# Decode attention over a 64K-key cache: earlier statistics for the second half of a pair, its accumulator in another bank, and one V load in halves

## The chip, the cores and the metric

The kernel runs on one core of a Trainium2 chip. The metric is device time in microseconds (us) from the first to the last instruction of an execution, as measured on the device; lower is better. One execution in each run is also recorded by the hardware profiler. Its span (660.0 us for the kernel before) is about 1.3 us shorter than that execution's time.

Engine names: PE is the matmul engine, DVE the vector engine, ACT the scalar engine, POOL the general engine, SP the engine that issues the DMAs here. PE's clock is throttled in some stages: 0.5 in the profile means half speed.

## The reference

One new token attends to a cache of 65,536 keys with 32 query heads that share 8 key/value heads; beside it runs a small dense layer, and both are added to the input.

```python
def _A_ref(x, k_cache, v_cache, wq, wo):        # x: (1, 1, 512); caches: (1, 8, 65536, 128) bf16
    q = (x @ wq) ...                            # 32 heads of 128
    k = jnp.repeat(k_cache, 4, axis=1); v = jnp.repeat(v_cache, 4, axis=1)
    scores = jnp.einsum("bhqd,bhkd->bhqk", q, k) * (128 ** -0.5)
    p = softmax(scores, axis=-1)
    o = jnp.einsum("bhqk,bhkd->bhqd", p, v)
    return o.transpose(...).reshape(...) @ wo
# out = x + _A_ref(layernorm(x), ...) + dense_gelu(layernorm(x), ...)
```

The caches are 268 MB, and each byte is used once for four query heads. All inputs together are 280.5 MB.

## The kernel before

The keys of one kv head are cut into four units of 16,384. Two units make a pair; there are 16 pairs, run as a rolled loop. One K chunk and one V chunk per pair, 8.4 MB each, come by DMA. K has two buffers. V has only one, of two halves ("Va" and "Vb"), so the V chunk of the next pair can be issued only when this pair's PV matmuls have read the old one.

```python
    for i in range(NU // 2):
        chunks += [("Ka", i), ("Kb", i)] if i in (0, LASTP - 1, LASTP) else [("K", i)]
        chunks += [("Va", i), ("Vb", i)] if i == LASTP else [("V", i)]
    chunks += [("W", 0)]                        # wo, the output projection
    ...
    def issue_chunks():                         # strictly in the order of the list
        while next_chunk[0] < len(chunks):
            ...
            if not need <= free:                # a buffer that it needs is still in use:
                return                          # nothing behind it is issued either
            ...                                 # one DMA; a POOL memset per half marks its landing ("flag")
```

One pair: 32 groups of 8 K tiles are transposed on PE, copied from PSUM to SBUF by DVE or ACT, and multiplied with q. Then come the row maxima over all keys ("statistics": two tiny matmuls with small DVE steps between), four exponentials on ACT with their sums, and the PV matmuls of both units.

```python
        for f in range(2 * FPU - LAG, 2 * FPU):
            scores(f)
        pv(2 * i, 0, 40)                # first unit's PV, tiles 0 to 39 of 128
        stats_1()                       # second unit's statistics, first matmul
        pv(2 * i, 40, 92)
        stats_2(2 * i + 1)              # second matmul, gives the negated maximum
        for j in range(HPG):
            weights(2 * i + 1, j)       # four exponentials on ACT, with sums
        keep_max(i)
        ...                             # (last pair only)
        pv(2 * i, 92, TPD)
        keep_sums(i)                    # DVE: the sums into one table
        total()                         # matmul with ones over all 128 columns of it
        ...                             # (last pair only)
        pv(2 * i + 1, 0, TPD)           # second unit's PV; then V's buffer is free
```

Both PVs accumulate in columns of one PSUM bank, `pO`. Because `keep_sums` waits for the four exponentials and `total` for `keep_sums`, PE stands still between the two PVs.

## Time and profile before

| | kernel before |
|---|---|
| median of 3 runs | 662.28 us (661.1 to 662.54) |
| profiled span | 660.0 us |
| load queue, share of 16 DMA engines' span | 98.8% |
| PE busy | 81% |
| usual time between two chunk landings | 19.36 us per 8.4 MB |

First, lines of the profile's page: the span; the engines' busy times; GB/s in 40 equal slices; and two DMA queues with their packets, MB and share of the 16 engines' span. q1 is the load queue, q8 brings instructions.

```profile
span 660.0 us, 29018 instructions
...
PE 535.0 (81%) x12682; PEld 509.0 (77%) x12682; DVE 280.4 (42%) x574; ACT 250.0 (38%) x454; POOL 5.6 (1%) x75
...
GB/s 388 439 463 415 369 445 409 417 445 445 445 441 385 445 445 445 445 417 409 445 445 437 441 409 429 445 433 433 409 441 421 433 437 425 421 445 413 425 441 271
...
q1 hardware_dynamic: 6600, 280.50, 98.8%
q8 instruction: 8, 0.13, 0.1%
...
```

The load queue is busy nearly all the time. The GB/s row tells more than the average: the fifth slice, 66 to 82 us, has 369, most others 409 to 445.

Next, POOL's timeline (start, duration, engine, line, operation, what ended the idle time before it). Each line marks the landing of a chunk.

```profile
...
80.49 0.12 POOL L454 MEMSET flag<- 1x1 bf16 x2 [19.22 <-DMA kv<-in_A_k_cache_dram]
101.61 0.12 POOL L454 MEMSET flag<- 1x1 bf16 x2 [20.99 <-DMA kv<-in_A_v_cache_dram]
...
509.30 0.12 POOL L454 MEMSET flag<- 1x1 bf16 x2 [19.23 <-DMA kv<-in_A_k_cache_dram]
529.83 0.12 POOL L454 MEMSET flag<- 1x1 bf16 x2 [20.41 <-DMA kv<-in_A_v_cache_dram]
549.20 0.12 POOL L454 MEMSET flag<- 1x1 bf16 x2 [19.24 <-DMA kv<-in_A_k_cache_dram]
...
```

V of pair 1 (the second line) came 21.1 us after K of pair 1, and V of pair 12 (at 529.83) came 20.5 us after the K chunk before it; the K chunk after it (549.20) came in the usual 19.37.

Then two V issues from SP's timeline, and one 5 us window (columns: length, busy time and instruction count of PE, PE weight load, DVE, ACT and POOL; PE clock; DMA share; GB/s).

```profile
...
79.84 0.33 SPq L449 DMA_DIRECT2D kv<-in_A_v_cache_dram  x1
...
505.69 0.33 SPq L449 DMA_DIRECT2D kv<-in_A_v_cache_dram  x1
...
```

```profile
...
75.00:80.00 5.00, 3.61 (x129) 3.47 (x127) 0.05 (x1) 0.00 (x0) 0.00 (x0) 0.50 0.61 257
...
```

V of pair 1 is issued at 79.84 us, when K of pair 1 is all but landed (80.49). Nothing else is queued, and the DMA share falls to 0.61. At 505.69 us the V issue is 3.6 us ahead of the K landing at 509.30.

PE's own waits (what waited, for what: us in total, times, longest), and the PV stage of pair 14 in PE's timeline:

```profile
...
PE pst L597 <- POOL flag L454: 65.9, 14, 6.8
PE pA L735 <- DVE sums_all L708: 19.3, 16, 1.2
...
```

```profile
...
608.68 0.35 PE L645 MATMUL pss<-q_cur,kt_ring 128*128 128x4 bf16 x8 [0.54 <-ACT kt_ring L636]
608.89 1.15 PE L718 MATMUL pO<-P_bf,kv 128*128 128x4 bf16 x40
609.98 0.59 PE L672 MATMUL pA<-ident_f,pmax 128*4 128x128 f32 x2
610.49 1.54 PE L718 MATMUL pO<-P_bf,kv 128*128 128x4 bf16 x52
611.97 0.59 PE L683 MATMUL pA<-diag,ones_f 4*128 4x4 f32 x2
612.49 1.12 PE L718 MATMUL pO<-P_bf,kv 128*128 128x4 bf16 x36
614.81 0.79 PE L735 MATMUL pA<-sums_all,ones_f 128*128 128x128 f32 x2 [1.20 <-DVE sums_all L708]
615.39 3.60 PE L718 MATMUL pO<-P_bf,kv 128*128 128x4 bf16 x128
...
```

PE waits 65.9 us for chunks, mostly for K, so the loads are the bound. Within a pair it waits 0.5 us for the last score tile's copy (line 608.68) and 1.2 us for the sums (line 614.81). The whole PV stage, from 608.89 to the end of the last matmul at 619.0, takes 10.1 us.

### The profile page before, as it was taken

What the parts mean: (1) busy time and instruction counts of PE and PEld (TensorE: products, weight loads), DVE (VectorE), ACT (ScalarE), POOL (GpSimd) and SP (SyncE); (2) the same over time, 40 slices, a digit from 0 to 9 for tenths busy, and PEclk for the clock granted to TensorE, in tenths of its full rate; (3) what the DMA queues carried; (4) which work ended last, traced back from release to release, by engine and by line L of the source; (5) the groups of instructions that cost most, each with busy time, mean ns of one, the idle gap of its engine ahead of it and who ended that gap; (6) DMA issues with size and microseconds to landing.
All of it is one profiled execution on the core that took longest, in us unless ns stands there. A gap on an engine that the chain in (4) does not pass through costs nothing. (4 is left out here: it accounts for less than half of the span.)

```text
span 660.0 us, 29018 instructions
## 1 busy us (share of the span) xinstructions
PE 535.0 (81%) x12682; PEld 509.0 (77%) x12682; DVE 280.4 (42%) x574; ACT 250.0 (38%) x454; POOL 5.6 (1%) x75
## 2 busy tenths in 40 slices
PE   2488498696969879697987959888696986999997
PEld 0277497696959879697987959788696986999997
DVE  3245063352615436162543616345261633536363
ACT  0144053352614425152442515345161543535261
POOL 0000000000000000000000000000000000000000
PEclk9689597795968769596886959679595976969695
DMA  9999899999998999999999999999999999999996
GB/s 388 439 463 415 369 445 409 417 445 445 445 441 385 445 445 445 445 417 409 445 445 437 441 409 429 445 433 433 409 441 421 433 437 425 421 445 413 425 441 271
DMA packets 6759, 280.66 MB, mean 425 GB/s; under 512 B 858, under 2 KB 1372, under 8 KB 1500
## 3 DMA queue, kind: packets, MB, share of 16 engines
q1 hardware_dynamic: 6600, 280.50, 98.8%
q8 instruction: 8, 0.13, 0.1%
q10 hardware_dynamic: 148, 0.01, 0.0%
q14 instruction: 3, 0.02, 0.0%
HBM read 280.50 MB, written 0.00 MB: 425 GB/s over the span
## 5 line engine op out<-in xcount | busy, mean ns | idle before, releaser
L597 PE MATMUL pst<-ident_bf,kv 128*128 128x128 bf16 x4096 | 336.6, 233 | 69.3 <-POOL flag L454 65.9
L597 PEld LDWEIGHTS pst<-ident_bf,kv 128*128 x4096 | 262.8, 105 | 71.4 <-issue 71.2
L636 ACT ACTIVATE kt_ring<-pst 128x1024 bf16<-128x1024 bf16 x192 | 196.7, 1025 | 310.9 <-PE pst L597 294.7
L634 DVE COPY kt_ring<-pst 128x1024 bf16<-128x1024 bf16 x320 | 216.8, 691 | 200.3 <-PE pst L597 200.2
L645 PE MATMUL pss<-q_cur,kt_ring 128*128 128x4 bf16 x4096 | 173.1, 165 | 10.9 <-ACT kt_ring L636 8.6
L645 PEld LDWEIGHTS pss<-q_cur,kt_ring 128*128 128x128 bf16 x4096 | 154.0, 97 | 16.2 <-ACT kt_ring L636 10.0
L718 PEld LDWEIGHTS pO<-P_bf,kv 128*128 128x128 bf16 x4096 | 115.5, 102 | 12.6 <-issue 11.3
L718 PE MATMUL pO<-P_bf,kv 128*128 128x4 bf16 x4096 | 118.4, 166 | 6.2 <-issue 6.2
L696 ACT ACTIVATE P_bf<-pss,negm 128x128 bf16<-128x128 f32 x128 | 57.2, 544 | 69.5 <-DVE negm L686 69.5
L728 DVE COPY o_all<-pO 128x4 f32 (+1 forms) x32 | 5.2, 162 | 77.8 <-PE pO L718 77.0
L696 ACT ACTIVATION_READ_ACCUMULATOR P_bf<-pss,negm 128x1 f32 x128 | 35.0, 273 | 0.0
L653 DVE TENSOR_REDUCE pmax<-pss 128x4 f32<-128x512 f32 x32 | 21.9, 686 | 25.2 <-PE pss L645 25.2
L735 PE MATMUL pA<-sums_all,ones_f 128*128 128x128 f32 x32 | 12.7, 501 | 19.3 <-DVE sums_all L708 19.3
L735 PEld LDWEIGHTS pA<-sums_all,ones_f 128*128 128x128 f32 x32 | 8.0, 311 | 20.6 <-DVE sums_all L708 20.6
L686 DVE TENSOR_SCALAR negm<-pA 128x4 f32<-128x4 f32 x32 | 5.0, 157 | 26.8 <-PE pA L683 26.8
L672 PE MATMUL pA<-ident_f,pmax 128*4 128x128 f32 x64 | 13.6, 299 | 1.3
L683 PE MATMUL pA<-diag,ones_f 4*128 4x4 f32 x64 | 14.3, 291 | 0.0
L674 DVE TENSOR_REDUCE gmax<-pA 4x1 f32<-4x128 f32 x32 | 8.8, 274 | 11.6 <-PE pA L672 11.6
L683 PEld LDWEIGHTS pA<-diag,ones_f 4*128 4x128 f32 x64 | 11.5, 223 | 1.9
L526 PE MATMUL pA<-ones_bf,xn_row 1*128 1x1 bf16 x4 | 0.3, 174 | 12.4 <-DVE xn_row L522 12.4
L526 PEld LDWEIGHTS pA<-ones_bf,xn_row 1*128 1x128 bf16 x4 | 0.2, 116 | 12.4 <-DVE xn_row L522 12.4
L454 POOL MEMSET flag<- 1x1 bf16 x64 | 4.2, 91 | 641.0 <-DMA kv<-in_A_k_cache_dram 327.7
(78 smaller groups left out, 60.2 us busy)
## 6 DMA issues: line engine op xcount, KB each, us to landing
kv<-in_A_k_cache_dram SPq DMA_DIRECT2D x6, 4096.0 KB, 36.6
kv<-in_A_v_cache_dram SPq DMA_DIRECT2D x2, 4096.0 KB, 26.3
kv<-in_A_wq_dram SPq DMA_DIRECT2D x1, 4096.0 KB, 12.5
kv<-in_B_w_dram SPq DMA_DIRECT2D x2, 1792.0 KB, 17.9
kv<-in_A_wo_dram SPq DMA_DIRECT2D x1, 2048.0 KB, 33.0
kv<-in_A_wo_dram SPq DMA_DIRECT2D x1, 1024.0 KB, 35.1
kv<-in_A_wo_dram SPq DMA_DIRECT2D x1, 512.0 KB, 35.8
kv<-in_A_wo_dram SPq DMA_DIRECT2D x1, 384.0 KB, 36.3
```

Source lines behind the costliest of these rows:

```text
L597: ins = pe.transpose(pst[tb][:, at * 128:(at + 1) * 128], kslot[0][:, t, :], ident_bf[:, :]).ins
L634: e, fn = DVE, lambda tb=tb, dst=dst: dve.tensor_copy(out=dst, in_=pst[tb][:, :])
L636: e, fn = ACT, lambda tb=tb, dst=dst: act.activation(out=dst, in_=pst[tb][:, :], func=ACTF.Copy)
L645: lambda k=k, kb=kb, at=at, t=t: pe.matmul(pss[k][:, at:at + HPG], lhsT=kt_ring[:, kb * FCOL + t * 128:kb * FCOL + (t + 1) * 128], rhs=q_c ...
L653: lambda k=k: dve.tensor_reduce(out=pmax[:, :], in_=pss[k][:, 0:CW].rearrange("p (t j) -> p j t", j=HPG), axis=AX.X, op=ALU.max),
L672: sch.op(PE, lambda: pe.matmul(pA[0:HPG, PA_ST:PA_ST + 128], lhsT=pmax[:, 0:HPG], rhs=ident_f[:, :], start=True, stop=True), reads=["pmax" ...
L674: sch.op(DVE, lambda: dve.tensor_reduce(out=gmax4[:, :], in_=pA[0:HPG, PA_ST:PA_ST + 128], axis=AX.X, op=ALU.max), reads=["pA"], writes=[" ...
L683: sch.op(PE, lambda: pe.matmul(pA[:, PA_SB:PA_SB + HPG], lhsT=ones_f[0:HPG, 0:128], rhs=diag4[0:HPG, 0:HPG], start=True, stop=True), reads ...
L696: lambda: act.activation(out=P_v[k][:, :, j], in_=src[:, :, j], func=ACTF.Exp, bias=negm[:, at:at + 1], scale=1.0, accum_out=sums[:, at:at ...
L718: lambda k=k, t=t: pe.matmul(pO[:, os], lhsT=vslot[:, k * TPD + t, :], rhs=P_v[k][:, t, :], start=t == 0, stop=t == TPD - 1),
L728: sch.op(DVE, lambda: dve.tensor_copy(out=o_all[:, at_pair(i, PW, k * HPG, HPG)], in_=pO[:, os]), reads=[f"pO{k}"], writes=[f"o{k}"])
L735: sch.op(PE, lambda: pe.matmul(pA[:, PA_SUM:PA_SUM + NC], lhsT=ones_f[:, :], rhs=sums_all[:, :], start=True, stop=True), reads=["ones_f", ...
```

## The change

The intent is to end a pair sooner on PE, so that V's buffer is free sooner, and to close the gap at the second V chunk:

- The second unit's statistics run at tiles 24 and 48 of the first PV instead of 40 and 92, so the exponentials are done when the first PV ends.
- The second PV accumulates in another bank (`pA`) and starts at once. The sums are totalled per pair by a matmul of 8 columns instead of 128, placed behind 32 tiles of the second PV.
- V of pair 1 comes in halves, so that its first half can be issued after the first PV of pair 0.
- The copy of the last score tile goes to DVE instead of ACT.

```diff
-        chunks += [("Va", i), ("Vb", i)] if i == LASTP else [("V", i)]
+        chunks += [("Va", i), ("Vb", i)] if i in (1, LASTP) else [("V", i)]
 ...
-        if f % 8 in (0, 2, 3, 5, 6):
+        if f % 8 in (0, 2, 3, 5, 7):            # these copies on DVE, the others on ACT
 ...
     def pv(u, t0, t1):
+        acc, res = ((pO, "pO0"), (pA, "pA"))[k]
 ...
-                    pO[:, os], lhsT=vslot[:, k * TPD + t, :], rhs=P_v[k][:, t, :],
+                    acc[:, 0:HPG], lhsT=vslot[:, k * TPD + t, :], rhs=P_v[k][:, t, :],
 ...
-    def total():
-        sch.op(PE, lambda: pe.matmul(pA[:, PA_SUM:PA_SUM + NC], lhsT=ones_f[:, :], rhs=sums_all[:, :], ...
+    def total(i):
+        sch.op(PE, lambda: pe.matmul(pO[:, PO_SUM:PO_SUM + PW], lhsT=ones_f[:, :], rhs=sums[:, :], ...
+        keep_o(i, 0)                            # DVE: first unit's result out of pO
+        sch.op(DVE, lambda: dve.tensor_copy(out=tot_all[:, ...], in_=pO[:, PO_SUM:PO_SUM + PW]), ...
 ...
-        pv(2 * i, 0, 40)
+        pv(2 * i, 0, 24)
         stats_1()
-        pv(2 * i, 40, 92)
+        pv(2 * i, 24, 48)
         stats_2(2 * i + 1)
 ...
-        pv(2 * i, 92, TPD)
-        keep_sums(i)
-        total()
+        pv(2 * i, 48, TPD)
+        pv(2 * i + 1, 0, 32)
+        total(i)
 ...
-        pv(2 * i + 1, 0, TPD)
+        pv(2 * i + 1, 32, TPD)
```

The rest of the diff (cut) passes exact semaphore growth per turn to the code that rolls the loop, and renames the table of sums.

More of the change, by code (lines that the diff above doesn't have):

```diff
@@ L152, in dma, with _fold @@
         return ev
-def _fold(bodies):
+def _fold(bodies, each):
     n = len(bodies)
@@ L164, in _fold @@
                 seen.setdefault((k, s), {})[i] = v
-    growth = {}
+    growth = dict(each)
     for (_, s), at in seen.items():
         if n - 1 in at and n - 2 in at:
-            growth.setdefault(s, at[n - 1] - at[n - 2])
+            assert growth.setdefault(s, at[n - 1] - at[n - 2]) == at[n - 1] - at[n - 2]
     out = []
@@ L193, in _emit, with _emit_rolled @@
             ins.then_inc(pub[0], pub[1])
-def _emit_rolled(eng_obj, ops, marks, holder=None, step=None):
-    folded, growth = _fold([ops[a:b] for a, b in zip(marks, marks[1:])])
+def _emit_rolled(eng_obj, ops, marks, each, holder=None, step=None):
+    folded, growth = _fold([ops[a:b] for a, b in zip(marks, marks[1:])], each)
     _emit(eng_obj, ops[:marks[0]])
@@ L369, in bass_parallel_sum__gqa_block_cached__dense_activation_gelu__decode_kernel @@
     negm_all = sb("negm_all", [128, NC], F32)
-    sums_all = sb("sums_all", [128, NC], F32)
+    tot_all = sb("tot_all", [128, NC], F32)
     o_all = sb("o_all", [128, NC], F32)
@@ L394, in bass_parallel_sum__gqa_block_cached__dense_activation_gelu__decode_kernel @@
     PA_ST = 128
-    PA_SUM = 384
+    PO_SUM = HPG
     csem = [sch.dsem(f"csem{i}") for i in range(6)]
@@ L404, in bass_parallel_sum__gqa_block_cached__dense_activation_gelu__decode_kernel @@
     sem_out = sch.dsem("dout")
-    sch.op(POOL, lambda: pool.memset(sums_all[:, :], 1.0), writes=["sums_all"])
     for t, res in ((ident_bf, "ident_bf"), (ident_f, "ident_f")):
@@ L705, in keep_max @@
                reads=["negm0", "negm1"], writes=["negm_all"])
-    def keep_sums(i):
-        sch.op(DVE, lambda: dve.tensor_copy(out=sums_all[:, at_pair(i, PW, 0, PW)], in_=sums[:, :]),
-               reads=[f"sums{at}" for at in range(PW)], writes=["sums_all"])
     def pv(u, t0, t1):
@@ L713, in pv @@
         x = "ab"[k]
-        os = slice(k * HPG, (k + 1) * HPG)
+        acc, res = ((pO, "pO0"), (pA, "pA"))[k]
         for t in range(t0, t1):
@@ L718, in pv @@
                 lambda k=k, t=t: pe.matmul(
-                    pO[:, os], lhsT=vslot[:, k * TPD + t, :], rhs=P_v[k][:, t, :],
+                    acc[:, 0:HPG], lhsT=vslot[:, k * TPD + t, :], rhs=P_v[k][:, t, :],
                     start=t == 0, stop=t == TPD - 1),
-                reads=[f"V{i}{x}"] + [f"P{k}_{j}" for j in range(HPG)], writes=[f"pO{k}"],
+                reads=[f"V{i}{x}"] + [f"P{k}_{j}" for j in range(HPG)], writes=[res],
                 publish=t == TPD - 1,
@@ L727, in pv, with keep_o @@
         done_chunk(f"V{x}")
-        sch.op(DVE, lambda: dve.tensor_copy(out=o_all[:, at_pair(i, PW, k * HPG, HPG)], in_=pO[:, os]),
-               reads=[f"pO{k}"], writes=[f"o{k}"])
+        if k:
+            keep_o(i, k)
+    def keep_o(i, k):
+        acc, res = ((pO, "pO0"), (pA, "pA"))[k]
+        sch.op(DVE, lambda: dve.tensor_copy(out=o_all[:, at_pair(i, PW, k * HPG, HPG)], in_=acc[:, 0:HPG]),
+               reads=[res], writes=[f"o{k}"])
     def by_head(t, a, b):
         return t[:, a * GW:b * GW].rearrange("p (g c j) -> p g j c", c=CPG, j=HPG)
-    def total():
-        sch.op(PE, lambda: pe.matmul(pA[:, PA_SUM:PA_SUM + NC], lhsT=ones_f[:, :], rhs=sums_all[:, :],
-                                     start=True, stop=True), reads=["ones_f", "sums_all"], writes=["pA_sum"])
+    def total(i):
+        sch.op(PE, lambda: pe.matmul(pO[:, PO_SUM:PO_SUM + PW], lhsT=ones_f[:, :], rhs=sums[:, :],
+                                     start=True, stop=True),
+               reads=["ones_f"] + [f"sums{at}" for at in range(PW)], writes=["pO0"])
+        keep_o(i, 0)
+        sch.op(DVE, lambda: dve.tensor_copy(out=tot_all[:, at_pair(i, PW, 0, PW)], in_=pO[:, PO_SUM:PO_SUM + PW]),
+               reads=["pO0"], writes=["tot_all"])
     def heads(t, a, b):
@@ L750, in weigh_2 @@
     def weigh_2():
-        sch.op(DVX, lambda: dve.tensor_tensor(out=wtot[:, :], in0=coef[:, :], in1=pA[:, PA_SUM:PA_SUM + NC],
-                                              op=ALU.mult), reads=["coef", "pA_sum"], writes=["wtot"])
+        sch.op(DVX, lambda: dve.tensor_tensor(out=wtot[:, :], in0=coef[:, :], in1=tot_all[:, :],
+                                              op=ALU.mult), reads=["coef", "tot_all"], writes=["wtot"])
         sch.op(DVX, lambda: dve.tensor_reduce(out=heads(rden, 0, G), in_=by_head(wtot, 0, G), axis=AX.X,
@@ L822, in bass_parallel_sum__gqa_block_cached__dense_activation_gelu__decode_kernel @@
         sch.reads.setdefault(res, []).extend(sch.reads["va"])
-    for res in ("K1a", "K1b", "Va", "Vb", "pO0", "pO1"):
+    for res in ("K1a", "K1b", "Va", "Vb", "pO0"):
         sch.reads.setdefault(res, []).append(made)
@@ L837, in bass_parallel_sum__gqa_block_cached__dense_activation_gelu__decode_kernel @@
         assert not (DVE.pending or ACT.pending)
+        was = {e.sem: e.count for e in (PE, DVE, ACT)}
         body(i)
+        each = {e.sem: e.count - was[e.sem] for e in (PE, DVE, ACT)}
     marks.append(len(PE.ops))
@@ L902, in _ @@
         def _(e):
-            _emit_rolled(e, ACT.ops, [m[1] for m in marks2])
+            _emit_rolled(e, ACT.ops, [m[1] for m in marks2], each)
         @block.vector
         def _(e):
-            _emit_rolled(e, DVE.ops[:rest[DVE]], [m[0] for m in marks2], pair)
+            _emit_rolled(e, DVE.ops[:rest[DVE]], [m[0] for m in marks2], each, pair)
         @block.tensor
@@ L911, in _ @@
             k_setup()
-            _emit_rolled(e, PE.ops[:rest[PE]], marks, step=k_step)
+            _emit_rolled(e, PE.ops[:rest[PE]], marks, each, step=k_step)
     for e, obj in ((PE, pe), (DVE, dve), (SP, sp)):
```

## The prediction

> **What bounds it now.** The DMA stream. The queue table puts the load queue at 98.8% of 16 engines' span, 280.5 MB. The K/V flags (timeline of the flag memsets, set when each 8.4 MB chunk lands) mostly come every 19.36 us, 433 GB/s. The Trainium skill, "DMA: Bandwidth & Descriptors", Specifications, gives a 435 GB/s fabric ceiling; the trace agrees. So the bytes alone cost about 647 us (estimate). PE is 81% busy but waits for a flag in 14 of 16 pairs (waits view: 65.9 us), so its time matters only where it delays a DMA issue, and in the last three pairs, which it runs almost without a break.
>
> **Where the stream loses time.**
> 1. Once it runs dry. V of pair 1 is issued at 79.84 us, when pair 0's PV has ended (SP timeline); K1 lands at 80.44; in 75 to 80 us the DMA share is 0.61 (windows view). V1's flag comes at 101.61, 1.6 us late for the last DMA engine, up to 3.6 us for others. Pair 0's PV is slow because PE stands still 5.0 us at 66 us and 1.2 us at 77 us ("issue"). My reading is instruction fetch in the loop's first turn (the skill, "Runtime: NRT & Kernel Launch", Instruction fetch mechanics, describes fetches by DMA and stalls on them; the trace shows the stall, not its cause).
> 2. Four later V chunks take 19.8 to 20.6 us (flags at 334, 374, 530, 609): 3.5 us together. Their V issues were only 3.5 to 4.3 us ahead of the K landing; issues 5 us ahead show no such loss.
>
> **What the change does.**
> - V1a can be issued after pair 0's first PV (near 73 us, estimate). The gap of point 1 should go: 1.5 us.
> - With statistics at 24 and 48, the exponentials (1.6 us for four) end before the second PV. PE's 1.2 us wait on sums per pair (waits view: 19.3 us in 16) goes. The sum matmul shrinks from 128 to 8 columns (now 0.8 us; perhaps 0.35 less). The last score tile's copy moves from ScalarE (1.02 us) to VectorE (0.69): about 0.3 us off a 0.54 us wait. Against it: about 0.3 us of short waits before statistics, one more small copy. Net, PE ends a pair 1.2 to 1.5 us earlier.
> - In the steady state that becomes longer PE waits for K and V issues about 5 us ahead. I expect half to most of point 2 back: 2.2 us.
> - In the tail, PE (three pairs of 35 us from K13's landing at 549) gains about 4 us, so it no longer binds; the end stays about 2.5 us after the last wo piece lands (657.46 us). The tail gains only what the stream gained.
>
> **Predicted:** 662.3 - 1.5 - 2.2 = 658.6 us, range 656.0 to 661.3. Faster by over 2%: 0.02; within 2%: 0.97; slower: 0.01.
>
> **What would show it.** V1's flags half a chunk apart, the second near 99.9 us; DMA share in 75 to 80 us near 1. PE's wait at the sum matmul gone; the second PV following the first unbroken. PE's wait for K flags up by about 1.2 us per pair, rather than the span down by 16 x 1.2. Later V flags at 19.36 us steps. Last wo landing earlier by as much as the span.
>
> **What would make it wrong.** If the late losses don't come from late V issues, they stay and the gain is 1.5 us. If V1a queued early lengthens pair 0's fetch stall, the gap only moves. If statistics at tile 24 stall PE over 1.2 us, or the folded loop's waits become stricter, pairs get no shorter. If the moved accumulator adds a wait, the tail gives a little back.

## The result, and the profile after

| | before | after |
|---|---|---|
| median of 4 runs each | 662.41 us (661.1 to 664.63) | 655.95 us (655.7 to 656.39) |
| ratio | | 0.990, 95% interval 0.9872 to 0.9927 |
| profiled span | 660.0 us | 654.7 us |
| load queue's share | 98.8% | 99.4% |

A ratio is the mean time of one kernel's runs over that of the other's runs of the same rounds, so it is not quite the ratio of the medians quoted beside it.

The direction and the class (within 2%) were as predicted. The time was not: 655.95 us lies just under the range (656.0 to 661.3), and the gain was 6.5 us instead of 3.7.

The page after:

```profile
span 654.7 us, 29020 instructions
...
GB/s 385 444 428 438 419 447 434 436 424 444 436 424 424 444 436 428 424 444 440 420 436 433 440 424 440 424 444 432 432 420 448 436 424 428 422 454 410 432 432 303
...
q1 hardware_dynamic: 6744, 280.50, 99.4%
...
```

POOL's timeline, with V of pair 1 now in two lines (90.47 and 100.19):

```profile
...
80.76 0.12 POOL L453 MEMSET flag<- 1x1 bf16 x2 [19.23 <-DMA kv<-in_A_k_cache_dram]
90.47 0.09 POOL L453 MEMSET flag<- 1x1 bf16 x1 [9.59 <-DMA kv<-in_A_v_cache_dram]
100.19 0.09 POOL L453 MEMSET flag<- 1x1 bf16 x1 [9.63 <-DMA kv<-in_A_v_cache_dram]
...
506.55 0.12 POOL L453 MEMSET flag<- 1x1 bf16 x2 [19.22 <-DMA kv<-in_A_k_cache_dram]
525.89 0.12 POOL L453 MEMSET flag<- 1x1 bf16 x2 [19.23 <-DMA kv<-in_A_v_cache_dram]
...
```

V of pair 1 takes two steps of 9.7 us, and V of pair 12 lands at 525.89, 19.34 us after K. The V issues and the window:

```profile
...
72.61 7.87 SPq L448 DMA_DIRECT2D kv<-in_A_v_cache_dram  x2
...
501.22 0.33 SPq L448 DMA_DIRECT2D kv<-in_A_v_cache_dram  x1
...
```

```profile
...
75.00:80.00 5.00, 1.49 (x54) 1.49 (x54) 0.00 (x0) 0.00 (x0) 0.00 (x0) 0.50 0.95 403
...
```

The first line of SP covers two issues, V1's first half at 72.61 and its second half at 80.15. The DMA share in 75 to 80 us is 0.95 instead of 0.61. At 501.22 us the V issue is now 5.3 us ahead of the K landing at 506.55; it was 3.6.

PE's waits, and the PV stage of pair 14:

```profile
...
PE pst L596 <- POOL flag L453: 81.9, 15, 7.0
...
PE pA L671 <- DVE pmax L652: 2.7, 15, 0.2
...
```

```profile
...
603.53 0.80 PE L713 MATMUL pO<-P_bf,kv 128*128 128x4 bf16 x24 [1.54 <-POOL flag L453]
604.26 0.58 PE L671 MATMUL pA<-ident_f,pmax 128*4 128x128 f32 x2
604.78 0.80 PE L713 MATMUL pO<-P_bf,kv 128*128 128x4 bf16 x24
605.51 0.59 PE L682 MATMUL pA<-diag,ones_f 4*128 4x4 f32 x2
606.03 2.29 PE L713 MATMUL pO<-P_bf,kv 128*128 128x4 bf16 x80
608.18 0.99 PE L713 MATMUL pA<-P_bf,kv 128*128 128x4 bf16 x32
609.03 0.57 PE L735 MATMUL pO<-sums,ones_f 128*128 128x8 f32 x2
609.46 2.70 PE L713 MATMUL pA<-P_bf,kv 128*128 128x4 bf16 x96
...
```

The second PV (608.18) follows the first without a break, and the wait for the sums is gone. What is new is a wait of 0.2 us for the maxima in each pair (2.7 us in all). The stage takes 8.6 us, from 603.53 to 612.16. From the first transpose of a pair to its last PV matmul PE takes 32.9 us in the median of pairs 3 to 15, against 34.6. PE did not use these 1.7 us to go faster as a whole: its wait for chunks grew from 65.9 to 81.9 us.

Where the 5.3 us of the two profiled spans come from can be read from the landings of the last of the 16 DMA engines (semaphore events in the trace, in us; they are 0.05 earlier than POOL's flags):

| event | before | after | gained in this stretch |
|---|---|---|---|
| K of pair 1 | 80.44 | 80.71 | -0.27 |
| V of pair 1 | 101.56 | 100.14 | 1.69 |
| V of pair 14 | 608.62 | 603.34 | 3.86 |
| last piece of wo | 657.46 | 652.20 | -0.02 |
| end of the span | 660.0 | 654.7 | 0.0 |

The whole gain is lost streaming time won back. Up to V of pair 1 it is 1.4 us, and 3.9 us in the stretch of the later V chunks (3.8 of it in V steps longer than 19.355 us). The tail behind the last landing is 2.5 us in both.

### The profile page after: what moved, and what is told of

It reads as the page before. It is cut to its first block, busy times and chain, and to the rows that moved or that the text cites. A ratio compares the mean times of both kernels' runs of the same rounds, so it can differ in the third digit from the quotient of the medians.

```text
span 654.7 us, 29020 instructions
## 1 busy us (share of the span) xinstructions
PE 532.5 (81%) x12682; PEld 506.2 (77%) x12682; DVE 281.6 (43%) x574; ACT 249.9 (38%) x454; POOL 5.6 (1%) x74
## 3 DMA queue, kind: packets, MB, share of 16 engines
q1 hardware_dynamic: 6744, 280.50, 99.4%
## 4 chain that ended last, share of the span: by engine, by line
DMA 56%; PE 33%; DVE 3%; another core or an unknown queue 3%; ACT 2%; issue 2%; SPq 1%; POOL 0%; ACTq 0%; DVEq 0%
DMA kv<-in_A_k_cache_dram 40%; PE pst L596 16%; DMA kv<-in_A_v_cache_dram 9%; DMA kv<-in_A_wo_dram 6%; PE pss L644 5%; PE pA L713 4%; PE pO L713 4%; DVE pmax L652 1%; DMA rows_bf<-in_A_x_dram 1%; PE pA L671 1%; ACT kt_ring L635 1%; PE pA L682 1%; DVE kt_ring L633 1%; PE pO L532 1%
## 5 line engine op out<-in xcount | busy, mean ns | idle before, releaser
L596 PE MATMUL pst<-ident_bf,kv 128*128 128x128 bf16 x4096 | 335.9, 233 | 85.0 <-POOL flag L453 81.9
L713 PE MATMUL pO<-P_bf,kv 128*128 128x4 bf16 x2048 | 60.7, 166 | 5.8 <-issue 4.3
L713 PEld LDWEIGHTS pO<-P_bf,kv 128*128 128x128 bf16 x2048 | 56.9, 101 | 11.1 <-issue 9.1
L713 PEld LDWEIGHTS pA<-P_bf,kv 128*128 128x128 bf16 x2048 | 60.2, 106 | 4.6 <-issue 3.6
L713 PE MATMUL pA<-P_bf,kv 128*128 128x4 bf16 x2048 | 59.4, 166 | 4.4 <-issue 3.5
L728 DVE COPY o_all<-pO 128x4 f32 (+1 forms) x16 | 2.6, 161 | 54.5 <-PE pO L735 54.5
L728 DVE COPY o_all<-pA 128x4 f32 (+1 forms) x16 | 2.6, 161 | 38.2 <-PE pA L713 38.2
```

Of the source, the lines that this page charges most:

```text
L596: ins = pe.transpose(pst[tb][:, at * 128:(at + 1) * 128], kslot[0][:, t, :], ident_bf[:, :]).ins
L713: lambda k=k, t=t: pe.matmul(acc[:, 0:HPG], lhsT=vslot[:, k * TPD + t, :], rhs=P_v[k][:, t, :], start=t == 0, stop=t == TPD - 1),
```

## The experiments

Three theories were put against each other.

- LEAD: a V chunk that is issued too shortly before the first of the 16 DMA engines runs dry costs streaming time. "Lead" below is the time from V's issue to the moment when the first engine has finished the K chunk ahead of it. A shorter pair on PE matters only because it makes the lead longer.
- SPREAD: the gap at V of pair 1 lines the 16 engines up (they then land within 0.5 us of each other; without the gap, within 2.2), and a later loss on one engine shows only when they are lined up.
- PE-TIME: the last three pairs run on PE without a break, and the gain is PE work taken out of them.

Eleven runs were made, three or four to a call: nine other kernels, and each of the two kernels once more. All gave correct results. The three calls ran on three different chips, so times of different calls are compared with care. In each call the kernel before was timed on the same chip; its medians were 660.5, 662.36 and 663.03 us.

### First call (kernel before: 660.5 us, 7 runs)

**e1: V of pair 1 in halves, nothing else.** Edit to the kernel before:

```diff
-        chunks += [("Va", i), ("Vb", i)] if i == LASTP else [("V", i)]
+        chunks += [("Va", i), ("Vb", i)] if i in (1, LASTP) else [("V", i)]
```

> The kernel before with V1 alone in halves; every other operation as before. All theories: V1's second half lands about 1.4 us earlier (near 100.1 us). LEAD theory (late losses come because V is issued only 1.6 to 4 us before the first DMA engine runs dry; V1's halves do not change that): the late V chunks still lose some 3 us together, time about 661, gain 1.4. SPREAD theory (the gap at V1 lines all 16 engines up, so that a later loss on any one engine is a loss of the whole; without the gap the engines stay 2.2 us apart and such losses hide behind the last one): late losses mostly hidden, time 657 to 658, gain 4 to 5.

Measured: 659.54 us (658.82 to 664.73), ratio 1.0001 (0.9952 to 1.005). The gap closed as planned: the second half landed at 100.06 us. But V chunks from pair 2 on lost 3.0 us on the last engine. LEAD is supported: with the engines 2 us apart, most of the losses still showed. Hiding as SPREAD has it does exist. In V of pairs 6, 11, 13 and 14 the middle engine lost 0.3 to 0.9 us and the last at most 0.05; the mean engine lost 3.8 us in all. But hiding did not save the 4 to 5 us that SPREAD expected, and it is not what the changed kernel gains by: there the mean engine lost 0.0 us, so nothing was left to hide. There is a lesson in the first of the losses. The gap had pushed everything behind it back by more than it delayed PE, so that V of pair 2 had 6.0 us of lead in the kernel before. With the gap closed it had 1.55 us, and lost 0.7 us at once. One of the later ones, V of pair 9, in SP's and POOL's timelines:

```profile
...
388.66 0.33 SPq L449 DMA_DIRECT2D kv<-in_A_v_cache_dram  x1
...
```

```profile
...
392.61 0.12 POOL L454 MEMSET flag<- 1x1 bf16 x2 [19.52 <-DMA kv<-in_A_k_cache_dram]
412.96 0.12 POOL L454 MEMSET flag<- 1x1 bf16 x2 [20.23 <-DMA kv<-in_A_v_cache_dram]
...
```

V is issued 3.9 us before K's flag (1.95 us before the first engine runs dry) and lands 20.35 us after it, 1.0 us late.

**e2: the changed kernel with V of pair 1 whole.**

```diff
-        chunks += [("Va", i), ("Vb", i)] if i in (1, LASTP) else [("V", i)]
+        chunks += [("Va", i), ("Vb", i)] if i == LASTP else [("V", i)]
```

> The changed kernel with V1 whole again. The gap at V1 returns (about 1.4 us on the last engine) and the engines are lined up. LEAD theory: V issues stay 5 us or more ahead of the K landing, so no late losses: about 657.4, i.e. 1.4 over the changed kernel. SPREAD theory: single engines still lose now and then and it now shows: 658.5 to 660.

Measured: 659.54 us (656.32 to 661.19), ratio 0.9964 (0.9929 to 0.9999). The number misses LEAD's 657.4 and falls into SPREAD's range, so the profile has to decide. It shows that LEAD's time was too low because the gap itself was far larger in this execution:

```profile
...
82.79 0.33 SPq L448 DMA_DIRECT2D kv<-in_A_v_cache_dram  x1
...
```

```profile
...
80.46 0.12 POOL L453 MEMSET flag<- 1x1 bf16 x2 [19.24 <-DMA kv<-in_A_k_cache_dram]
104.75 0.12 POOL L453 MEMSET flag<- 1x1 bf16 x2 [24.16 <-DMA kv<-in_A_v_cache_dram]
...
```

V was issued 2.3 us after K had landed, and landed 24.3 us after it, a loss of 4.9 us. After that, with the engines lined up within 0.5 us and leads of 4.5 to 7.8 us, V chunks lost 0.3 us in all (0.4 in one chunk, at a lead of 5.15; that one LEAD does not explain). SPREAD had expected losses here, and the profile shows almost none. The halves of V of pair 1 are therefore worth 1.4 us in one profiled execution and 4.9 in another, by how long pair 0 takes. A gap that varies so would account for the wide spread of this kernel's runs, 5 us against 0.7 for the changed kernel; only one of the four was profiled, so this is not shown.

**e3: the kernel before with all V chunks but the first in halves.** PE's work is untouched.

```diff
-        chunks += [("Va", i), ("Vb", i)] if i == LASTP else [("V", i)]
+        chunks += [("Va", i), ("Vb", i)] if i > 0 else [("V", i)]
```

> The kernel before with every V chunk but the first in halves: the first half is issued when the first PV is done, some 5 us earlier, with PE's own work untouched. LEAD theory: no gap, no late loss, 655.5 to 656.7, the same as the changed kernel although PE still waits 1.2 us for the sums in every pair. PE-TIME theory (the gain is PE work taken out of a chain that PE binds, as in the last three pairs): 658 or more, since PE's pairs are as long as before.

Measured: 656.9 us (656.68 to 657.26), ratio 0.994 (0.992 to 0.996). SP's timeline shows why: the first half is issued 5.4 us before the second (its first line is a second half, its second line both halves of the next chunk).

```profile
...
503.60 0.33 SPq L449 DMA_DIRECT2D kv<-in_A_v_cache_dram  x1
...
536.80 5.71 SPq L449 DMA_DIRECT2D kv<-in_A_v_cache_dram  x2
...
```

```profile
...
507.33 0.12 POOL L454 MEMSET flag<- 1x1 bf16 x2 [19.27 <-DMA kv<-in_A_k_cache_dram]
517.04 0.09 POOL L454 MEMSET flag<- 1x1 bf16 x1 [9.59 <-DMA kv<-in_A_v_cache_dram]
526.75 0.09 POOL L454 MEMSET flag<- 1x1 bf16 x1 [9.62 <-DMA kv<-in_A_v_cache_dram]
...
```

No V chunk from pair 2 on lost anything beyond 0.1 us. The second halves of pairs 2 to 14 were issued 1.5 to 3.0 us before K's first engine ran dry, which is when a whole V would have been issued; with the first half already queued, that short lead cost nothing (503.60 and 526.75 in the lines of pair 12). PE's wait for the sums was still there in full:

```profile
...
PE pA L735 <- DVE sums_all L708: 19.2, 16, 1.2
...
```

This is the sharpest of the runs. One line of code that gives V's loads more lead, with PE's own work unchanged, takes 3.6 us off the median of the kernel before in this call. (The changed kernel was not timed in this call; its medians elsewhere, 655.8 to 655.95 us, are 1 us lower, about what the added chunk boundaries cost, see e8.) The time is 0.2 us above LEAD's range and 1.1 below PE-TIME's 658. PE-TIME as the main cause is refuted.

**e4: the changed kernel with 12 extra matmuls per pair.** Their results are not used; they take 1.44 us.

```diff
-        pv(2 * i + 1, 32, TPD)
+        pv(2 * i + 1, 32, 96)
+        for r in range(12):
+            sch.op(PE, lambda: pe.matmul(pO[:, 256:384], lhsT=ident_bf[:, :], rhs=ident_bf[:, :], start=True, stop=True),
+                   reads=["ident_bf"], writes=["pO0"], publish=False)
+        pv(2 * i + 1, 96, TPD)
```

> The changed kernel with 12 idle-making matmuls (128x128 identity, results unused) in each second PV, estimated at 1.3 us at the low clock, so that PE's pair and V's issue are about where they were before. V1's halves stay. LEAD theory: V is issued 1.7 to 3.2 us ahead of the first dry engine, some late losses return: 657 to 659. SPREAD theory: they hide, within 0.6 us of the changed kernel. PE-TIME theory: the last three pairs add 3 x 1.3 us, about 659 or more.

Measured: 658.24 us (656.92 to 661.64), ratio 0.9973 (0.9935 to 1.001). PE's pair was 34.2 us, nearly that of the kernel before, and the leads fell to 1.7 to 3.8 us. The late losses came back in part (1.1 us on the last engine in the profiled execution), and so did the spread between runs. This is what LEAD expected. By its median alone it lies near PE-TIME's "about 659" too, and the tail behind the last landing grew from 2.5 to 2.9 us; e9 tells the two apart.

### Second call (kernel before: 662.36 us, 7 runs, 659.89 to 665.0)

**r1: the changed kernel again**, as a yardstick. No edit.

> The changed kernel itself on the chip of this call, as the yardstick for the two below. Expected 655.5 to 656.7; every V chunk from the third on lands in 19.35 us steps.

Measured: 655.77 us (655.63 to 655.96), ratio 0.9898 (0.9859 to 0.9937). Leads were 3.6 to 4.9 us, and no V chunk from pair 2 on lost anything.

**r2: a second profile of the kernel before.** No edit.

> A second profile of the kernel before, to see whether what it loses differs between executions. LEAD theory: V chunks with less than about 3 us between V's issue and the first DMA engine running dry again land late, but not the same ones as in the first profile; the sum of all losses over 19.35 us steps explains the difference of the two spans. If losses sat at the same chunks whatever the lead, something else in the program would cause them.

Measured: 661.86 us, span 660.5 us. Its late V chunks lost 3.6 us in all, but mostly in other places: V of pairs 6, 8, 9, 11 and 13 instead of 7, 8, 12 and 14. Their leads were 1.8 to 2.9 us. The losses belong to short leads more than to places in the program, and their places differ from one execution to the next. The other expectation failed: the V losses do not explain that this span is 0.5 us longer, for they are 0.2 us smaller; a K step was 0.3 us longer, and the tail was 2.9 us instead of 2.5. Both profiled executions lost about the same sum, so they do not show why the kernel before scatters over 5 us. What points to the leads is which kernels scatter: those with short leads or the gap (before, e1, e2, e4, e5) over 4.4 to 5.9 us, those with long leads (after, r1, e3, e8, e9) over 0.9 at most; e6 and e7, in between, over 1.9 and 1.6.

**e5: 24 extra matmuls per pair**, the edit of e4 with 24 for 12.

> The changed kernel with 24 extra matmuls in each second PV (2.9 us at the low clock, by the 1.44 us that 12 took). LEAD theory: V is issued only 0 to 1.7 us ahead of the first dry engine, nearly every V chunk loses about 1 us or more: 665 to 675, far more than twice the loss of 12. PE-TIME theory (only the last three pairs count): 3 x 2.9 us over the changed kernel at most, about 661 to 664.

Measured: 662.7 us (660.29 to 664.72), ratio 1.0006 (0.9956 to 1.0057). The direction is right and the size was wrong: I expected 665 to 675, and the time falls into PE-TIME's range of 661 to 664. The profile shows that PE's tail is the smaller part. Its span is 5.5 us longer than the changed kernel's: V chunks of pairs 2 to 14 lost 3.0 us on the last engine, K chunks 1.6 us, and the tail behind the last landing is 0.75 us longer (3.2 instead of 2.45). The K losses are not explained by LEAD, since these chunks were issued over 20 us ahead; losses of K also came, smaller, in e1 (0.4 us) and r2 (0.3), and none over 0.1 us in after, r1, e3, e8 and e9. V of pair 2 had a lead of -0.5 us and lost 1.2 us, but all later V together lost only 1.8 us. My reading is that the loss is its own remedy: a late V pushes the next K back, PE then starts later, and the next pair issues its V with more lead. The leads fit: after -0.52, 1.45, 0.87 and 1.45 us the next ones were 3.4, 2.1, 2.7 and 2.0. As long as a pair on PE (35.4 us here) is shorter than its two chunks (38.7 us), the leads should not fall for good.

**e9: all V chunks in halves and 12 extra matmuls**, the edits of e3 and e4 on the changed kernel.

> The changed kernel with all V chunks but the first in halves, and the same 12 extra matmuls (1.44 us per pair) that cost about 2 us in the run with 12. LEAD theory: the first half is issued 5 us earlier, so the extra PE work costs nothing until the tail: 656.0 to 657.3, tight runs. PE-TIME theory: as with 12 extra matmuls, 658 or more.

Measured: 657.13 us (656.6 to 657.46), ratio 0.9917 (0.9877 to 0.9956). The same extra PE work that gave 658.2 us and 4.7 us of scatter gives 657.1 us and 0.9 us when the lead is long. The stream lost nothing (from V of pair 1 to V of pair 15 it took 543.06 us, as in e3 and e8), and the tail was 2.9 us instead of 2.5: PE time as such costs 0.4 us here, at the end.

### Third call (kernel before: 663.03 us, 7 runs)

**e6: the last score tile's copy back on ACT.**

```diff
-        if f % 8 in (0, 2, 3, 5, 7):
+        if f % 8 in (0, 2, 3, 5, 6):
```

> The changed kernel with the last score tile's copy back on ScalarE (and the tile before it on VectorE). PE's pair should be about 0.3 us longer, the lead of V's issue over the first dry engine 2.7 to 4.2 us instead of 3.0 to 4.6. LEAD theory with a threshold near 3 us: at most one or two small losses, 655.6 to 656.6.

Measured: 656.07 us (655.8 to 657.67), ratio 0.9895 (0.9864 to 0.9926). The wait for the last score tile's copy was back at 0.54 us (PE's timeline, pair 14). Three of four executions took 655.8 to 656.3 us. The profiled one is the fourth: V of pair 2 had a lead of only 1.5 us there, after a slow pair 0, and lost 1.7 us.

**e7: statistics back at tiles 40 and 92**, the rest as changed.

```diff
-        pv(2 * i, 0, 24)
+        pv(2 * i, 0, 40)
         stats_1()
-        pv(2 * i, 24, 48)
+        pv(2 * i, 40, 92)
         ...
-        pv(2 * i, 48, TPD)
+        pv(2 * i, 92, TPD)
```

> The changed kernel with the second unit's statistics back at tiles 40 and 92 of the first PV; the accumulator, the small sum matmul behind tile 32, the copies and V1's halves as changed. The second PV must now wait for the exponentials, about 1.2 us per pair, so the lead falls to 1.8 to 3.4 us. LEAD theory: late losses like those with 12 extra matmuls (658.2), 656.5 to 658.8. If instead the small sum matmul or the bank were what counted, it would stay at 655.8.

Measured: 656.62 us (656.15 to 657.71), ratio 0.9909 (0.9877 to 0.9942). The second PV now waits for the exponentials, 1.0 us in each pair:

```profile
...
PE pA L713 <- ACT P_bf L695: 15.0, 15, 1.0
...
```

The leads were 2.2 to 3.9 us; small losses on single engines came back, most of them hidden behind the last engine. So of what the change takes out of a pair, 1.0 us is the earlier statistics, up to 0.5 us the copy (e6), and the rest the smaller sum matmul and its wait. (The waits are the better measure here: the median length of a pair on PE was 32.9 us in one profile of the changed kernel and 32.2 in the other, whose mean granted clocks were 0.786 and 0.793.) Against r1, which ran on another chip, undoing either part alone cost under 1 us of time, where the lead stays near the threshold below.

**e8: the changed kernel with all V chunks but the first in halves**, to see whether more lead still wins.

> The changed kernel with all V chunks but the first in halves: the largest lead of all. If lead were still short in the changed kernel this would be under 655.5. LEAD theory: nothing is left to win, and the kernel before with all halves (656.9) showed that twice as many chunk boundaries cost about 1 us: 656.2 to 657.2.

Measured: 656.87 us (656.72 to 656.97), ratio 0.9908 (0.9877 to 0.9939). More lead wins nothing, and each extra chunk boundary costs about 0.08 us (from V of pair 1 to V of pair 15 it is 543.07 us between landings, against 542.05 in r1 on another chip, with 13 more boundaries; e3 has the same 543.06). No version beat the changed kernel.

### The threshold

The whole V chunks of pairs 2 to 14 in the ten profiles with whole V chunks (before twice, after twice, e1, e2, e4, e5, e6, e7) give 130 cases. A loss is what the step from K's to V's landing has beyond 19.355 us; in the third column it is that of the middle of the 16 engines, in the fourth a chunk counts when its first, middle or last engine lost over 0.1 us.

| lead, us | chunks | mean loss, middle engine, us | with a loss |
|---|---|---|---|
| under 1 | 2 | 1.54 | 2 |
| 1 to 2 | 14 | 0.52 | 14 |
| 2 to 2.5 | 13 | 0.24 | 12 |
| 2.5 to 3 | 21 | 0.11 | 10 |
| 3 to 3.5 | 26 | 0.01 | 5 |
| over 3.5 | 54 | 0.00 | 5 |

The loss fades out near 3 us of lead rather than ending at a sharp value. The leads of the kernel before were 1.6 to 6.0 us in its first profile, those of the changed kernel 3.0 to 4.6. Lead does not account for all of the 3.8 us that the first profile lost: V of pairs 7 and 8 had leads of 3.0 and 3.3 us and lost 0.5 and 0.6 us on the last engine (0.1 in the mean of the 16), while six chunks of the changed kernel with leads of 3.0 to 3.4 us lost nothing on the last engine. Over V of pairs 2 to 14 the mean engine of that profile lost 1.9 us; the rest of the 3.8 is the last engine falling behind the others, from 0.5 to 3.0 us after the first. The DMA packets in the trace show where such a threshold can come from. When V of pair 1 was issued into an empty queue, its first packets started 0.96 us after the issue (before: issue 79.84, first packet 80.80, last engine's first packet 81.60; e2: 82.79, 83.75 and 84.42), and the first packet on an engine then took mostly 2.8 to 3.4 us where later ones take 2.42. In sum the chunk landed as if the full stream had begun 2.4 us (before) and 2.6 us (e2) after the issue. V of pair 12 in the kernel before, issued 2.06 us ahead (mean loss of the 16 engines 0.8 us), paid a part of both: around it an engine was without a packet for 0.4 us on average, and its packets together took 0.5 us more than 2.42 us each (the longest 4.05 us). This was summed for this one chunk only, and what makes the packets slow stays open.

## Why the prediction was right or wrong

- **DMA bound, and the span ends 2.5 us after wo's last piece.** Right: 657.46 to 660.0 before, 652.20 to 654.7 after.
- **V of pair 1 in halves, 1.5 us.** Right for the profiled execution (the landing moved from 101.56 to 100.14). The size varies: e2 shows 4.9 us in an execution with a slower pair 0. The cause that I gave, instruction fetch in the loop's first turn, fits every stall. In three traces (before, after, e2) each of PE's "issue" stalls over 1 us in pair 0 ends 1.2 to 1.6 us after a 16,384-byte packet of the instruction queue (before: packets end at 59.92, 69.43 and 76.70 us, PE goes on at 61.21, 71.03 and 78.23). No run took the fetches away, so this stays a strong coincidence. The Trainium skill, "Runtime: NRT & Kernel Launch", Instruction fetch mechanics, states refills in 16 KiB blocks over DMA; the packet size agrees.
- **PE's pair shorter by 1.2 to 1.5 us.** A little low: 1.7 us in the two first profiles. The wait for the sums went as predicted, the score copy's wait fell from 0.5 to at most 0.2 us per pair, and the new waits for maxima are 0.2 us.
- **PE's wait for chunks up by 1.2 us per pair instead of a faster span.** Right: 65.9 to 81.9 us, 1.0 per pair.
- **"I expect half to most of point 2 back: 2.2 us".** This is the step that failed: the size of the won-back losses. The prediction had found 3.5 us of late losses and took off only 2.2, without a reason for the part. The profiled execution lost 3.8 us over V of pairs 2 to 14, and all of it came back; in both profiles of the changed kernel the losses sum to zero. The mechanism, V issued too shortly before the stream runs out, was right (e3, e9). The runs show losses that fade out near 3 us of lead: the change brought all leads to 3.0 us or more.
- **What I did not count at all.** I took the losses from one execution of 661.28 us and subtracted them from the median. The kernel before scatters from 659.85 to 665.0 us over all its runs; its median in the rounds with the changed kernel was 662.41, 1.1 us above the profiled execution. The changed kernel removes the scatter as well, so the medians differ by 6.5 us where the profiled executions differ by 5.3. The sum with the measured terms is 1.4 + 3.8 + 1.1 = 6.3 us. That the 1.1 us are more of the same losses is likely but not shown, since no execution at or above the median was profiled; that the profiled execution was quicker than the median is chance.
- **The two parts need each other.** I added their gains. Alone, the halves gave no clear gain (e1: interval 0.9952 to 1.005), and the rest gave 0.36% (e2); together they gave 1%. In e1's profile, closing the gap took away lead that the gap had given (V of pair 2: 1.55 us instead of 6.0); the shorter pair makes up for it.

What stays open: why chunks with leads over 3 us lost something in 10 of 80 cases, why K chunks lost something in e5, how far the losses explain the scatter, and what exactly fills the 3 us.

## What to carry to other kernels

When a stream of loads is the bound and a buffer is freed late, look for each chunk at how far ahead of the first engine running dry its load is issued, not at the average busy share: 98.8% busy hid 5 us here. Time saved on an engine that is not the bound was worth only the load losses that it took away: here it paid while leads were under about 3 us, and nothing beyond (e8). Issuing a chunk in two halves bought the lead with one line, at about 0.08 us per added chunk boundary. And take a loss that comes and goes from several executions, for a median can hold losses that one profile does not show.

## What the Trainium skill lacked or had wrong

- "DMA: Bandwidth & Descriptors", Specifications, gives a first-byte latency of about 0.6 us for DMAs issued from SP, and does not say from where it counts. Here the first packet of a load issued into an empty or nearly empty queue started 0.95 to 0.97 us after the start of SP's issuing instruction (before, e2, e5, r2); that instruction took 0.33 us, so from its end it is 0.62 to 0.64 us, which agrees. What this page lacks is the rest: an 8.4 MB load over 16 engines landed as if the full stream had begun 2.4 to 2.7 us after the issue.
- No page has how far ahead of the first engine running dry a load must be queued to lose next to nothing (about 3 us here), or that what is lost below this falls on different chunks in different executions of one kernel (before and r2).
- "DMA: Bandwidth & Descriptors", Where 436 GB/s comes from, says that for loads from HBM the HBM side (about 358 GB/s) binds. As a sentence by itself it misleads: with one core running this program, the case shows 433 GB/s over chunk after chunk (8.4 MB in 19.35 us), close to the page's fabric ceiling of 435. The page's own measurement for a single core, 425, fits this.
- No page gives the cost of a chunk boundary in a full queue; here it is about 0.08 us.
- "Runtime: NRT & Kernel Launch", Instruction fetch mechanics, calls the cost of crossing a 16 KiB block mostly hidden (it names a stall for taken branches). In the first turn of this loop, beside a full load queue, PE stood still 1.2 to 5.0 us at such blocks (5.0 us at 66 us of the kernel before), if the coincidence above is the cause.
